# Queries and keys of a sliding-window attention and gated FFN kernel: cast by DMA into 4 KB runs and turned in 32x32 blocks on VectorE

## The chip, the cores and the metric

One core of a Trainium2 chip. The metric is the device time of one execution in microseconds (us). A time is the median of several runs on one chip; the kernel before and the changed kernel were run in turn.

## The reference

Attention over q, k, v of shape (8 batches, 8 heads, 576 tokens, 64 channels) in float32, causal, with a window of 64 tokens; its output, laid out as 4608 tokens x 512 channels, goes through a gated FFN with 1536 hidden channels.

```python
scores = scale * q @ k.T                       # per batch and head
mask   = (rel >= 0) & (rel < 64)               # rel = query position - key position
attn   = softmax(where(mask, scores, -1e9))
x      = (attn @ v).transpose(0, 2, 1, 3).reshape(4608, 512)
out    = (silu(x @ w_gate) * (x @ w_val)) @ w_out
```

## The kernel before

The 4608 tokens are worked in nine tiles of 512 (the tiles cross batch borders, so a tile has one or two segments). The score matmuls read queries and keys with channels on partitions: `qT`, `kT` are 128 partitions (two heads of 64 channels, a "head pair" `u`) x 4 pairs x 512 tokens. The kernel gets there in four steps: SyncE loads float32 with two tokens per partition row, GpSimd casts, TensorE transposes 128x128 blocks against an identity into PSUM (the memory that TensorE's results go to in this kernel; one buffer of 128x512 float32 in it is called a bank here), and ScalarE and VectorE copy the result to SBUF (the memory of all its other tiles).

```python
def cast_qk(t):                                 # GpSimd, 8 casts of 128x512
    ...
def transposes(t, u):                           # 8 transposes on TensorE, 2 copies
    tp = ps_a.tile([P, 2, 512], BF16, name="tp", tag="a")
    ...
    nc.tensor.transpose(tv[:, i, g, e], x[:, g, e, 2*u:2*u+2, :]..., identb[:])
    ...
    nc.scalar.copy(outs[0], parts[0])           # qT
    nc.vector.tensor_copy(outs[1], parts[1])    # kT

def gate_value(t, m):                           # 12 of these per tile
    g_ps = ps_f.tile([P, 512], FP32, name="g_ps", tag="g")   # two buffers
    v_ps = ps_f.tile([P, 512], FP32, name="v_ps", tag="v")   # two buffers
    # 4 + 4 matmuls of 128x512
    nc.scalar.activation(sg[:], g_ps[:], AF.Silu)
    nc.vector.tensor_mul(hT[t][:, m, :], sg[:], v_ps[:])      # frees v_ps

for t in range(2, NT):
    if t > 2:
        loads_qk(t + 2); loads_v(t + 1)         # ends of the range cut
        # attention phase: products(t, u), scores(t + 1, u), project(t - 1, s)
    cast_qk(t + 2)
    for m in range(12):                         # gate/value stage
        gate_value(t, m)
        if m % 3 == 2:
            u = m // 3
            cast_v(t + 1, u)
            masks(t + 1, u)                     # on GpSimd
            transposes(t + 2, u)
```

VectorE runs its instructions in order: in after, an `hT` multiply whose inputs were done by 205.96 us starts at 209.75, behind the mask and the two transposes that stand before it in the program. And the multiply that writes `hT` is the only thing that frees a `v_ps` bank in the gate/value stage, and there are two such banks.

The softmax here doesn't subtract the row's maximum and nothing guards it: scores larger than these inputs give would overflow.

Of the kernel before, what the change touches and what calls it, by code (L numbers as in the profile page):

```python
# [8 lines left out]
P = 128  # L9
FP32 = mybir.dt.float32  # L10
BF16 = mybir.dt.bfloat16
# [6 lines left out]
def kernel(  # L18
# [10 lines left out]
    nc = tc.nc  # L29
    S, D, H = 576, 64, 8  # L30
    NTOK, DFF, DM = 4608, 1536, 512
    NT = NTOK // 512

    ctx.enter_context(tc.manual_schedule())
    cst = ctx.enter_context(tc.tile_pool(name="cst", bufs=1))
    stage = ctx.enter_context(tc.tile_pool(name="stage", bufs=2))
    cast = ctx.enter_context(tc.tile_pool(name="cast", bufs=1))
    att = ctx.enter_context(tc.tile_pool(name="att", bufs=2))
# [6 lines left out]
    wg = cst.tile([P, 4, DFF], BF16, name="wg")  # L45
    wv = cst.tile([P, 4, DFF], BF16, name="wv")
    wo = cst.tile([P, 12, DM], BF16, name="wo")
    kT = [cst.tile([P, 4, 512], BF16, name=f"kT{i}") for i in range(2)]
    vp = [cst.tile([P, 9, H, D], BF16, name=f"vp{i}") for i in range(2)]
    identb = cst.tile([P, P], BF16, name="identb")  # L50
    ones = cst.tile([P, D], BF16, name="ones")
# [2 lines left out]
    def segments(t):  # L54

        n0 = 64 * t
        segs = []
        if n0 > 0:
            segs.append((0, t - 1, S - n0, min(n0, 512)))
        if n0 < 512:  # L60
            segs.append((n0, t, 0, 512 - n0))
        return segs

    staged = {}
# [7 lines left out]
    def load_qk(eng, t, i, h=None):  # L72

        dst = staged[t][i]
        src = (q, k)[i]
        for off, b, s0, n in segments(t):
            o, s, left = off, s0, n
            while left:
                if h is not None and o % 256 == 0 and left >= 256:
                    m, r = left // 256 * 256, P  # L80
                else:
                    m = min(left, 256 - o % 256)
                    r = m // 2
                p0, g = o % 256 // 2, o // 256
                if h is None:
                    eng.dma_start(
                        dst[p0:p0 + r, g].rearrange("r h e d -> r h (e d)"),
                        src[b, :, s:s + m].rearrange("h (r e) d -> r h (e d)", e=2),
                    )
                else:  # L90
                    eng.dma_start(  # L91
                        dst[p0:p0 + r, g:g + max(1, m // 256), h].rearrange("r g e d -> r g (e d)"),
                        src[b, h, s:s + m].rearrange("(g r e) d -> r g (e d)", e=2, r=r),
                    )
                o, s, left = o + m, s + m, left - m

    def load_v(engs, t, by_head=False):

# [40 lines left out]
    def cast_qk(t):  # L139
        casts(t)  # L140
        for g in range(2):
            for e in range(2):
                for i in range(2):
                    cast_unit(nc.gpsimd, t, i, g, e=e)

    def cast_v(t, u):

        v_f = staged[t, "v"]
        hs = slice(2 * u, 2 * u + 2)
        if u == 0 and t:  # L150
            nc.gpsimd.tensor_copy(vp[t % 2][64:128, 0], vp[(t - 1) % 2][64:128, 8])
        for a in range(2):
            r = slice(64 * a, 64 * a + 64)
            dst = vp[t % 2][r, a:a + 8, hs, :].rearrange("r (i c) h d -> r i c (h d)", c=2)
            src = v_f[r, :, hs, :].rearrange("r i h d -> r i (h d)")
            nc.gpsimd.tensor_copy(  # L156
                dst, src.rearrange("r i (c x) -> r i c x", c=1).broadcast_to([64, 4, 2, P])
            )
# [13 lines left out]
    queries = {}  # L172

    def transposes(t, u):
        tp = ps_a.tile([P, 2, 512], BF16, name="tp", tag="a")
        tv = tp[:].rearrange("r i (g j e x) -> r i g e j x", g=2, j=4, e=2)
        for i, x in enumerate(ready[t]):
            for g in range(2):
                for e in range(2):
                    nc.tensor.transpose(  # L180
                        tv[:, i, g, e],
                        x[:, g, e, 2 * u:2 * u + 2, :].rearrange("r h d -> r (h d)"),
                        identb[:],
                    )
        if u == 0:
            queries[t] = att.tile([P, 4, 512], BF16, name="qT", tag="qT")
        parts = [tp[:, i, :].rearrange("r (j e x) -> r j e x", j=8, e=2) for i in range(2)]
        outs = [
            x[:, u, :].rearrange("r (j x e) -> r j e x", j=8, e=2)
            for x in (queries[t], kT[t % 2])  # L190
        ]
        nc.scalar.copy(outs[0], parts[0])  # L192
        nc.vector.tensor_copy(outs[1], parts[1])  # L193

    weights = {}

    def scores(t, u):

        qT = queries[t][:, u, :]
        E = epool.tile([P, 2, 512], BF16, name="E", tag="E")  # L200
        s_ps = [ps_a.tile([P, 512], FP32, name="s_ps", tag="a") for _ in range(2)]
        for j in range(-1 if t else 0, 8):
            c = j % 2
            lo, hi = max(0, 64 * j), min(512, 64 * j + P)
            src = kT[t % 2] if j >= 0 else kT[(t - 1) % 2]
            for h in range(2):
                r = slice(64 * h, 64 * h + 64)
                nc.tensor.matmul(  # L208
                    s_ps[h][64 * c:64 * c + 64, lo:hi],
                    src[r, u, 64 * (j % 8):64 * (j % 8) + 64],  # L210
                    qT[r, lo:hi],
                )
        for h in range(2):
            if t == 0:
                nc.vector.memset(E[64:128, h, 0:64], 0.0)
                nc.scalar.activation(E[0:64, h, 0:64], s_ps[h][0:64, 0:64], AF.Exp, scale=0.125)
            lo = 0 if t else 64
            nc.scalar.activation(E[:, h, lo:512], s_ps[h][:, lo:512], AF.Exp, scale=0.125)  # L218
        weights[t, u] = E

    def masks(t, u, eng=nc.gpsimd):

        E = weights[t, u]
        eng.tensor_mul(  # L224
            E[:].rearrange("r h x -> r (h x)"),
            E[:].rearrange("r h x -> r (h x)"),
            mask[:].rearrange("r h i c x -> r (h i c x)"),
        )
        if 0 < t < 8:
            a = 64 * (1 - t % 2)  # L230
            nc.gpsimd.memset(E[a:a + 64, :, 64 * t:64 * t + 64], 0.0)  # L231
# [41 lines left out]
    def project(t, s, eng=None):  # L273
        o_ps = ps_f.tile([P, 512], FP32, name="o_ps", tag="gv"[s % 2])
        for c in range(12):
            nc.tensor.matmul(  # L276
                o_ps[:], hT[t][:, c, P * s:P * s + P], wo[:, c, :],
                start=(c == 0), stop=(c == 11),
            )
        os_ = fsb.tile([P, 512], FP32, name="os_", tag="os_", bufs=2)  # L280
        if eng is None:
            nc.vector.tensor_copy(os_[:], o_ps[:])
        else:
            nc.scalar.copy(os_[:], o_ps[:])
        nc.sync.dma_start(out[512 * t + P * s:512 * t + P * s + P, :], os_[:])
# [7 lines left out]
    def loads_qk(t):  # L293
        stages(t)
        load_qk(nc.sync, t, 0)
        load_qk(nc.sync, t, 1)

    def loads_v(t):
        load_v((nc.sync, nc.sync), t)
# [62 lines left out]

    attention(1, rest)
    set_silu()
    loads_qk(2)
    loads_v(2)
    for m in range(3):
        gate_value(1, m)
    for s in range(1, 4):
        for t in range(2):  # L370
            for m in range(3 * s, 3 * s + 3):
                gate_value(t, m)
    loads_qk(3)
    loads_v(3)
    cast_qk(2)

    set_exp()
    for u in range(4):
        transposes(2, u)
        if u == 0:  # L380
            project(0, 0)
        scores(2, u)
        cast_v(2, u)
        masks(2, u, nc.vector)
        if u:
            project(0, u)
    cast_qk(3)
    loads_qk(4)
    for u in range(4):
        transposes(3, u)  # L390
        products(2, u)
        project(1, u)
        scores(3, u)
    set_silu()

    for t in range(2, NT):
        if t > 2:
            if t + 2 < NT:
                loads_qk(t + 2)
            if t + 1 < NT:  # L400
                loads_v(t + 1)
            set_exp()
            for u in range(4):
                products(t, u)
                if u % 2 == 0:
                    project(t - 1, u // 2)
            for u in range(4):
                if t + 1 < NT:
                    scores(t + 1, u)
                if u % 2 == 1:  # L410
                    project(t - 1, 2 + u // 2)
            set_silu()
        if t + 2 < NT:
            cast_qk(t + 2)
        for m in range(12):
            gate_value(t, m)
            if m % 3 == 2:
                u = m // 3
                if t + 1 < NT:
                    cast_v(t + 1, u)  # L420
                    masks(t + 1, u)
                if t + 2 < NT:
                    transposes(t + 2, u)
    for s in range(4):
        project(NT - 1, s)

# [29 lines left out]
```

## Time and profile before

| | before |
|---|---|
| median | 402.7 us |
| span of the profiled run | 400.5 us |
| TensorE busy | 352.9 us, 88% |
| VectorE / ScalarE / GpSimd busy | 41% / 48% / 46% |
| first gate matmul of tile 2 | 139.96 us |
| from there to the first gate matmul of tile 7 (five tiles) | 191.7 us, 38.3 each |

How to read the lines: L216 is line 216 of the kernel, an arrow points from what is read to what is written, and xN counts instructions. DVE is VectorE, ACT ScalarE, POOL GpSimd, PE TensorE, PEld its weight loads. The first lines are from the page of before: the span, TensorE's busy time with its share and instructions, and the chain of work that ended last, by engine and by line.

```profile
span 400.5 us, 7241 instructions
PE 352.9 (88%) x2872; PEld 173.4 (43%) x2872; DVE 165.9 (41%) x254; ACT 193.1 (48%) x314; POOL 186.0 (46%) x229
...
PE 76%; POOL 5%; issue 5%; DMA 5%; ACT 4%; SPq 3%; DVE 1%; POOLq 0%; DVEq 0%; ACTq 0%
```

So TensorE is both the busiest engine and three quarters of the chain. The table of windows of before says where it idles. Columns: stretch, its length, then busy us and instruction count of each engine, the granted clock of TensorE (1.00 is full speed), the DMA share and GB/s.

```profile
core 0: us, PE busy (x) PEld busy (x) DVE busy (x) ACT busy (x) POOL busy (x), PEclk, DMA share, GB/s
97.26:121.30 24.04, 16.63 (x162) 8.82 (x160) 9.04 (x13) 8.57 (x14) 11.54 (x18) 0.96 0.19 62
121.30:139.96 18.66, 18.66 (x217) 9.36 (x216) 8.01 (x12) 10.25 (x18) 3.72 (x7) 0.87 0.42 134
139.96:163.20 23.24, 23.24 (x155) 11.65 (x148) 10.82 (x16) 12.15 (x19) 19.58 (x21) 1.00 0.61 148
163.20:179.80 16.60, 15.51 (x183) 7.58 (x182) 6.17 (x9) 12.15 (x20) 13.28 (x17) 1.00 0.14 50
```

The first two rows are the transition from the opening tiles to the steady loop; the third is a gate/value stage, without a gap on TensorE; the fourth is an attention phase, with 1.1 us of gap. (The borders are rough: by the timeline this stage, with its last transposes, goes from 139.96 to 162.48 us, 22.5 us, and the phase to 178.30, 15.8 us.) Whatever leaves TensorE in the third row is saved time (the run packed below bears this out: 22.5 to 20.8 us per stage without the transposes).

The timeline of before, TensorE alone, shows what one group of transposes costs there (start, duration, what):

```profile
303.26 1.03 PE L265 MATMUL v_ps<-xT,wv 128*128 128x512 bf16 x4
304.12 0.39 PE L180 MATMUL tp<-identb,q_b 128*128 128x128 bf16 x4
304.35 0.39 PE L180 MATMUL tp<-identb,k_b 128*128 128x128 bf16 x4
304.57 1.03 PE L265 MATMUL g_ps<-xT,wg 128*128 128x512 bf16 x4
```

Read the starts, not the durations, which overlap: the next gate matmul starts 0.45 us later than it would without the eight transposes. Four groups are 1.8 us per tile.

### The profile page before, as it was taken

The numbers are of one execution on the slowest core, as the hardware profiler recorded it, in microseconds if no ns is written. First come the engines' busy times: TensorE is split into PE (matmuls) and PEld (weight loads), VectorE is DVE, ScalarE is ACT, GpSimd is POOL, SyncE is SP. The second block draws the span as 40 slices with busy tenths as digits, with TensorE's granted clock in tenths as the row PEclk, the third lists the DMA queues.
The fourth block names the chain that finished last, engine by engine and source line by source line (L and its number), as shares of the span: only waits on it lengthen the run. The fifth ranks groups of instructions, "written<-read, shape, count | busy, mean of one in ns | idle before, by whom it ended". The sixth has DMA issues, their size and how long they took to land.

```text
span 400.5 us, 7241 instructions
## 1 busy us (share of the span) xinstructions
PE 352.9 (88%) x2872; PEld 173.4 (43%) x2872; DVE 165.9 (41%) x254; ACT 193.1 (48%) x314; POOL 186.0 (46%) x229
## 2 busy tenths in 40 slices
PE   1368459999669999989999998999899989999996
PEld 0143233444324545445444554445445444444442
DVE  1563534444432544524452544254434433443432
ACT  0476455334424564674476447545663664363320
POOL 7932493200460399778078617952795049000000
PEclk9999559999997999999999999999999999999999
DMA  9693599992117194019212901490160011002002
GB/s 238 170 163 92 139 232 191 204 251 58 54 63 227 54 246 96 29 59 272 64 43 78 285 19 54 130 239 2 54 156 4 0 64 44 0 28 79 2 5 100
DMA packets 87154, 42.94 MB, mean 107 GB/s; under 512 B 40016, under 2 KB 82512, under 8 KB 87120
## 3 DMA queue, kind: packets, MB, share of 16 engines
q1 hardware_dynamic: 77040, 36.19, 34.2%
q0 software_dynamic: 5792, 4.72, 7.5%
q10 hardware_dynamic: 4288, 1.57, 1.5%
q8 instruction: 22, 0.36, 0.4%
q14 instruction: 12, 0.10, 0.1%
HBM read 37.75 MB, written 9.44 MB: 118 GB/s over the span
## 4 chain that ended last, share of the span: by engine, by line
PE 76%; POOL 5%; issue 5%; DMA 5%; ACT 4%; SPq 3%; DVE 1%; POOLq 0%; DVEq 0%; ACTq 0%
PE v_ps L265 23%; PE g_ps L265 23%; PE o_ps L276 22%; PE tp L180 3%; DMA v_f<-in_v_dram 3%; POOL vp L156 2%; PE ad_ps L241 2%; PE s_ps L208 2%; SPq L91 2%; PE ao_ps L245 2%; DMA k_f<-in_k_dram 2%; ACT ld L251 1%; ACT E L218 1%; SPq L109 1%; ACT L288 1%
## 5 line engine op out<-in xcount | busy, mean ns | idle before, releaser
L271 DVE TENSOR_TENSOR hT<-sg,v_ps 128x512 bf16<-128x512 f32 x108 | 74.3, 688 | 103.7 <-PE v_ps L265 101.0
L270 ACT ACTIVATE sg<-g_ps 128x512 f32<-128x512 f32 x108 | 64.4, 597 | 101.8 <-PE g_ps L265 99.7
L265 PE MATMUL g_ps<-xT,wg 128*128 128x512 bf16 x432 | 112.7, 383 | 0.8 <-DVE xT L254 0.8
L265 PE MATMUL v_ps<-xT,wv 128*128 128x512 bf16 x432 | 111.7, 381 | 0.0
L276 PE MATMUL o_ps<-wo,hT 128*128 128x512 bf16 x432 | 100.6, 385 | 0.0
L156 POOL CAST vp<-v_f 64x1024 bf16<-64x1024 f32 x72 | 75.4, 1047 | 16.1 <-DMA v_f<-in_v_dram 13.4
L224 POOL TENSOR_TENSOR E<-E,mask 128x1024 bf16<-128x1024 bf16 x24 | 51.0, 2124 | 32.1 <-ACT E L218 30.6
L265 PEld LDWEIGHTS <-wv 128*128 128x128 bf16 x432 | 42.4, 98 | 53.0 <-issue 2.6
L265 PEld LDWEIGHTS <-wg 128*128 128x128 bf16 x432 | 41.6, 98 | 47.9 <-issue 1.7
L276 PEld LDWEIGHTS <-hT 128*128 128x128 bf16 x432 | 40.2, 99 | 46.8 <-issue 2.5
L218 ACT ACTIVATE E<-s_ps 128x512 bf16<-128x512 f32 (+1 forms) x72 | 38.4, 589 | 24.1 <-PE s_ps L208 23.7
L192 ACT COPY qT<-tp 128x512 bf16<-128x512 bf16 x36 | 26.4, 734 | 39.0 <-PE tp L180 39.0
L132 POOL CAST q_b<-q_f 128x512 bf16<-128x512 f32 x28 | 17.2, 615 | 54.1 <-PE tp L180 30.2
L193 DVE COPY kT<-tp 128x512 bf16<-128x512 bf16 x36 | 26.4, 732 | 37.0 <-ACT qT L192 37.0
L254 DVE TENSOR_TENSOR xT<-ao_ps,r 128x512 bf16<-128x512 f32 x36 | 24.9, 692 | 30.8 <-ACT r L253 30.8
L180 PE MATMUL tp<-identb,q_b 128*128 128x128 bf16 x144 | 16.5, 234 | 15.9 <-POOL q_b L134 13.0
L251 ACT ACTIVATE ld<-ad_ps 128x512 f32<-128x512 f32 x36 | 21.5, 598 | 16.1 <-PE ad_ps L241 14.4
L208 PE MATMUL s_ps<-qT,kT 64*64 64x128 bf16 (+1 forms) x640 | 17.4, 233 | 9.8 <-ACT E L218 4.8
L180 PE MATMUL tp<-identb,k_b 128*128 128x128 bf16 x144 | 16.2, 239 | 11.0 <-DVE k_b L134 11.0
L231 POOL MEMSET E<- 64x128 bf16 x28 | 5.6, 202 | 41.6 <-DVE E L224 40.4
L253 ACT ACTIVATE r<-ld 128x512 f32<-128x512 f32 x36 | 22.7, 630 | 1.2
L180 PEld LDWEIGHTS <-q_b 128*128 128x128 bf16 x144 | 10.7, 101 | 24.4 <-POOL q_b L134 14.4
(65 smaller groups left out, 185.7 us busy)
## 6 DMA issues: line engine op xcount, KB each, us to landing
v_f<-in_v_dram SPq DMA_DIRECT2D x25, 256.0 KB, 5.2
q_f<-in_q_dram SPq DMA_DIRECT2D x9, 512.0 KB, 4.6
k_f<-in_k_dram SPq DMA_DIRECT2D x9, 512.0 KB, 6.2
v_f<-in_v_dram SPq DMA_DIRECT2D x12, 128.0 KB, 3.4
wg<-in_moe_w_gate_dram POOLq DMA_DIRECT2D x4, 384.0 KB, 9.5
wv<-in_moe_w_val_dram POOLq DMA_DIRECT2D x4, 384.0 KB, 11.5
wo<-in_moe_w_out_dram POOLq DMA_DIRECT2D x2, 768.0 KB, 24.3
q_f<-in_q_dram SPq DMA_DIRECT2D x11, 128.0 KB, 3.3
```

Source lines behind the costliest of these rows:

```text
L156: nc.gpsimd.tensor_copy(dst, src.rearrange("r i (c x) -> r i c x", c=1).broadcast_to([64, 4, 2, P]))
L180: nc.tensor.transpose(tv[:, i, g, e], x[:, g, e, 2 * u:2 * u + 2, :].rearrange("r h d -> r (h d)"), identb[:],)
L192: nc.scalar.copy(outs[0], parts[0])
L193: nc.vector.tensor_copy(outs[1], parts[1])
L208: nc.tensor.matmul(s_ps[h][64 * c:64 * c + 64, lo:hi], src[r, u, 64 * (j % 8):64 * (j % 8) + 64], qT[r, lo:hi],)
L218: nc.scalar.activation(E[:, h, lo:512], s_ps[h][:, lo:512], AF.Exp, scale=0.125)
L224: eng.tensor_mul(E[:].rearrange("r h x -> r (h x)"), E[:].rearrange("r h x -> r (h x)"), mask[:].rearrange("r h i c x -> r (h i c x)"),)
L251: nc.scalar.activation(ld[:], d_ps[:], AF.Ln)
L265: nc.tensor.matmul(ps[:], w[:, c, P * m:P * m + P], xT[t][:, c, :], start=(c == 0), stop=(c == 3),)
L270: nc.scalar.activation(sg[:], g_ps[:], AF.Silu)
L271: nc.vector.tensor_mul(hT[t][:, m, :], sg[:], v_ps[:])
L276: nc.tensor.matmul(o_ps[:], hT[t][:, c, P * s:P * s + P], wo[:, c, :], start=(c == 0), stop=(c == 11),)
```

## The change

The intent: take the transposes off TensorE, the casts and masks off GpSimd, and make the DMA runs long. From tile 2 on, GpSimd's DMA queue casts queries and keys to bf16 while it loads them. One partition gets a run of 16 tokens of one head (4 KB of float32). A 32x32 block transpose on VectorE then turns 32 partitions (32 token groups `x`) by 32 channels, once for each of the 16 tokens `e` of a run. Because a block transpose here takes only 32 channels of a run (`src[:, u, :, 0:32]`), each run is loaded twice, for the two channel halves `c`, the second time shifted by 32 elements. The masks move from GpSimd to VectorE.

```diff
+    def load_shifted(t):
+        both = [stage.tile([P, 4, 16, D], BF16, name=n, tag=n) for n in ("q_f", "k_f")]
+        ...
+        w = 16 * D - 32
+        for dst, src in zip(both, (q, k)):
+            for a in range(2):
+                for c in range(2):
+                    for off, b, s0, n in segments(t):
+                        p0 = 64 * a + 32 * c + off // 16
+                        x = src[b, a:H:2, s0:s0 + n].rearrange("u (r e) d -> r u (e d)", e=16)
+                        nc.gpsimd.dma_start(
+                            dst[p0:p0 + n // 16].rearrange("r u e d -> r u (e d)")[:, :, 0:w],
+                            x[:, :, 32 * c:32 * c + w],
+                        )
...
+    def turn(t, u):
+        ...
+        for src, dst in zip(staged[t], (queries[t], kT[t % 3])):
+            nc.vector.transpose(
+                dst[:, u, :].rearrange("r (x e) -> r e x", e=16), src[:, u, :, 0:32]
+            )
...
     for t in range(2, NT):
-                loads_qk(t + 2)
+                load_shifted(t + 2)
...
-            cast_qk(t + 2)
...
-                    masks(t + 1, u)
+                    masks(t + 1, u, nc.vector)
-                    transposes(t + 2, u)
+                    turn(t + 2, u)
```

(Cut: a third `kT` buffer, and the same exchange in the transition, where the four turns of tiles 2 and 3 stand in a row.)

More of the change, by code (lines that the diff above doesn't have):

```diff
@@ L47 @@
     wo = cst.tile([P, 12, DM], BF16, name="wo")
-    kT = [cst.tile([P, 4, 512], BF16, name=f"kT{i}") for i in range(2)]
+    kT = [cst.tile([P, 4, 512], BF16, name=f"kT{i}") for i in range(3)]
     vp = [cst.tile([P, 9, H, D], BF16, name=f"vp{i}") for i in range(2)]
@@ L95, in load_qk @@
                 o, s, left = o + m, s + m, left - m
+    def load_shifted(t):
+        both = [stage.tile([P, 4, 16, D], BF16, name=n, tag=n) for n in ("q_f", "k_f")]
+        staged[t] = both
+        w = 16 * D - 32
[9 more added lines that the diff above has]
+                        )
     def load_v(engs, t, by_head=False):
@@ L189, in transposes @@
             x[:, u, :].rearrange("r (j x e) -> r j e x", j=8, e=2)
-            for x in (queries[t], kT[t % 2])
+            for x in (queries[t], kT[t % 3])
         ]
@@ L193, in transposes @@
         nc.vector.tensor_copy(outs[1], parts[1])
+    def turn(t, u):
+        if u == 0:
+            queries[t] = att.tile([P, 4, 512], BF16, name="qT", tag="qT")
+        for src, dst in zip(staged[t], (queries[t], kT[t % 3])):
+            nc.vector.transpose(
+                dst[:, u, :].rearrange("r (x e) -> r e x", e=16), src[:, u, :, 0:32]
+            )
     weights = {}
@@ L204, in scores @@
             lo, hi = max(0, 64 * j), min(512, 64 * j + P)
-            src = kT[t % 2] if j >= 0 else kT[(t - 1) % 2]
+            src = kT[t % 3] if j >= 0 else kT[(t - 1) % 3]
             for h in range(2):
@@ L364 @@
     set_silu()
-    loads_qk(2)
+    load_shifted(2)
     loads_v(2)
@@ L372 @@
                 gate_value(t, m)
-    loads_qk(3)
-    loads_v(3)
-    cast_qk(2)
+        if s == 1:
+            load_shifted(3)
+            loads_v(3)
+        for u in range(4):
+            if s == 3:
+                cast_v(2, u)
+                turn(2, u)
     set_exp()
     for u in range(4):
-        transposes(2, u)
-        if u == 0:
-            project(0, 0)
         scores(2, u)
-        cast_v(2, u)
         masks(2, u, nc.vector)
-        if u:
-            project(0, u)
-    cast_qk(3)
-    loads_qk(4)
+        project(0, u)
+    load_shifted(4)
     for u in range(4):
-        transposes(3, u)
+        turn(3, u)
+    for u in range(4):
         products(2, u)
@@ L412 @@
             set_silu()
-        if t + 2 < NT:
-            cast_qk(t + 2)
         for m in range(12):
```

## The prediction

> **What bounds the kernel now.** The page: span 400.5 us, TensorE busy 352.9 us (88%); the chain that ended last is 76% TensorE, nearly all gate, value and output matmuls. The table of windows splits the idle: 97.3 to 121.3 us (first scores of tile 2, with projections) has TensorE busy 16.6 of 24.0 us; each later attention phase (163.2 to 179.8) idles 1.1 us, ended by ScalarE's exponentials; the gate/value stages idle nothing. So from 62 us on only work taken off TensorE, or waits in the 97 to 140 stretch, are worth time.
>
> **What the change removes.**
> - TensorE: 8 transposes per head pair from tile 2 on. In the timeline one such group delays the next gate matmul by 0.45 us (304.12 to 304.57), 1.8 us per tile. Tiles 4 to 8 lie in saturated stages: 5 x 1.8 = 9.0 us, all critical.
> - The transition 97.3 to 140.0 (42.7 us): its chain is cast, transpose, ScalarE copy (0.73), VectorE copy (0.73), scores, twice over, and a throttled projection (4.6 us instead of 2.76) after idling. New estimate: 2.2 us wait for the first two VectorE transposes, 4 x 3.1 (scores 0.4, project 2.7), 4 x 3.75 (products, project, scores), 1.5 us for products held by VectorE: 31 us. Gain 11.5 us.
> - GpSimd casts (0.61 us x8 per tile), ScalarE copies and GpSimd masks (2.12 us): off the critical path.
>
> **What it adds.**
> - VectorE: two 32x32-block transposes per head pair, 128x512, costed as the 512-element multiply, 0.69 us ([...]this trace has none yet), plus a 0.69 us mask. Per three gate/value units: 3 x 0.69 + 2.1 = 4.1 us of 5.2. A value eviction is late by about 2 us; two banks absorb it.
> - DMA: queries and keys are read twice (about 4 MB f32 per tile for 2 MB), in 1024 runs of 4 KB. The weight loads, the only cast DMA now, show 5792 packets in 7.5% of 16 engines, 83 ns for 1.5 to 2 KB read; I estimate 160 to 200 ns per 4 KB run, 10 to 13 us per tile of all engines, beside 6 us of values. [...]an issue costs about 0.75 us here, at most eight are in flight by semaphore, 16 per tile. Issue begins with an attention phase; the first transpose is due 16.6 + 5.2 = 21.8 us later. I expect landing after 17 to 22 us: just in time. VectorE runs in order, so a late load holds hT, then TensorE.
>
> **Prediction.** 402.75 - 9.0 - 11.5 + 2 (some late loads) = about 384 us; 8 in 10 between 377 and 397. Faster by over 2% 0.83, within 2% 0.13, slower 0.04.
>
> **What would show it.** Right: transposes 0.6 to 0.75 us; gate/value stages of tiles 2 to 6 take 20.8 us instead of 22.5; second projections start near 111 us; TensorE busy near 337 us, idle 45. Wrong: VectorE's transpose line waits for DMA; TensorE gaps in gate/value stages released by hT; GpSimd held between DMA issues so that tile 2's value casts or mask memsets come after 111 us.
>
> **What would make it wrong.** Runs over 200 ns[...]; block transposes over 1.1 us; doubled reads delaying tile 2 beyond 97 us, as DMA is saturated 50 to 90 us already.

The 0.69 us was an estimate, from the multiply of 512 elements in the trace of before (0.688 us, mean of 108). What the traces show of the rest: the throttled projection (122.36 us in before) ran at a granted clock of 0.59, one of 2.76 us (128.43) at 1.00. An issue took 0.74 to 0.79 us in before (51.62 to 55.28 us). Of the 16 issues from 121.82 us in after, eight go out in a row in 4.06 us, a ninth at 125.95, and each of the other seven waits 0.29 to 1.14 us for a `q_f` load to land. The 6 us of values are near what after shows: a DMA share of 0.91 from 200 to 206 us, 5.5 us by this product, while a tile's values are loaded.

## More of the kernel before

The experiments ran in three groups on three chips (the kernel before took 402.8, 403.4 and 402.0 us there), so a difference between experiments of different groups is good to about 1 us.

## The result, and the profile after

| | before | after |
|---|---|---|
| median of 4 runs each | 402.69 us | 454.52 us |
| span | 400.5 us | 451.2 us |
| TensorE busy | 352.9 us, 88% | 348.8 us, 77% |
| VectorE busy | 165.9 us, 41% | 276.8 us, 61% |
| first gate matmul of tile 2 | 139.96 us | 153.02 us |
| from there to tile 7's, per tile | 38.3 us | 45.9 us |

The ratio is 1.129 (95% interval 1.125 to 1.133). Ratios here are the mean time of one kernel's fast runs over that of the other's of the same rounds, so they are not quite the ratio of the medians quoted. Of the 50.7 us of span, 13.1 came before tile 2's first gate matmul, 37.8 in the five tiles after it, and nothing after that.

The page of after, the same lines:

```profile
span 451.2 us, 6787 instructions
PE 348.8 (77%) x2607; PEld 162.8 (36%) x2648; DVE 276.8 (61%) x306; ACT 173.1 (38%) x286; POOL 161.1 (36%) x253
...
PE 38%; DVE 20%; issue 19%; DMA 15%; POOL 3%; SPq 2%; ACT 1%; DVEq 0%; ACTq 0%; POOLq 0%
```

TensorE has half the share of the chain that it had, and VectorE has 20% of it. The 19% under "issue" belong largely to VectorE as well: in the chain between 203 and 213 us the two long pieces of that name (206.02 to 207.59 and 207.75 to 209.75) lie inside its two transposes. The 15% of DMA are no sign of late loads: they are 16% in the run packed below, which is fast. The groups of after (busy us and mean ns of one, then the idle time of the engine just before them and what ended it):

```profile
L290 PE MATMUL v_ps<-xT,wv 128*128 128x512 bf16 x429 | 114.9, 391 | 27.2 <-DVE hT L296 27.0
L216 DVE STREAM_TRANSPOSE kT<-k_f 128x512 bf16<-128x512 bf16 x28 | 70.5, 2519 | 0.0
L216 DVE STREAM_TRANSPOSE qT<-q_f 128x512 bf16<-128x512 bf16 x28 | 67.1, 2396 | 0.0
```

The transposes take 2.4 to 2.5 us each by their records, not 0.69. They never wait: the idle time before them is 0.0, so the loads are not late. And value matmuls now wait 27 us for `hT`. One third of a gate/value stage in the timeline of after shows how (VectorE and TensorE, two stretches of rows; the last bracket is the idle time before and what ended it):

```profile
204.34 0.69 DVE L296 TENSOR_TENSOR hT<-sg,v_ps 128x512 bf16<-128x512 f32 x1 [1.04 <-PE v_ps L290]
...
204.94 0.69 DVE L249 TENSOR_TENSOR E<-E,mask 128x1024 bf16<-128x1024 bf16 x1
...
205.55 2.39 DVE L216 STREAM_TRANSPOSE qT<-q_f 128x512 bf16<-128x512 bf16 x1
...
207.59 2.49 DVE L216 STREAM_TRANSPOSE kT<-k_f 128x512 bf16<-128x512 bf16 x1
...
209.75 1.44 DVE L296 TENSOR_TENSOR hT<-sg,v_ps 128x512 bf16<-128x512 f32 x2
210.66 1.02 PE L290 MATMUL v_ps<-xT,wv 128*128 128x512 bf16 x4 [2.11 <-DVE hT L296]
...
212.39 0.68 DVE L249 TENSOR_TENSOR E<-E,mask 128x1024 bf16<-128x1024 bf16 x1
```

From 204.94 to 209.75 us VectorE does a mask and two transposes, and no `v_ps` bank comes free. TensorE fills both banks and then stands still for 2.11 us. From mask to mask the third takes 7.45 us; three units of eight matmuls need 5.18. VectorE is busy for 6.86 of the 7.45 us, so its own work alone exceeds the 5.18: by this sum more banks would not have saved the stage (no run tried it). By starts, which is the honest measure for instructions whose records overlap, a transpose costs 2.04 and 2.16 us.

### The profile page after: what moved, and what is told of

It is laid out like the page before. It is cut to its first block, busy times and chain, and to the rows that moved or that the text cites. A ratio compares the mean times of both kernels' runs of the same rounds, so it can differ in the third digit from the quotient of the medians.

```text
span 451.2 us, 6787 instructions
## 1 busy us (share of the span) xinstructions
PE 348.8 (77%) x2607; PEld 162.8 (36%) x2648; DVE 276.8 (61%) x306; ACT 173.1 (38%) x286; POOL 161.1 (36%) x253
## 4 chain that ended last, share of the span: by engine, by line
PE 38%; DVE 20%; issue 19%; DMA 15%; POOL 3%; SPq 2%; ACT 1%; DVEq 0%; ACTq 0%; POOLq 0%
PE o_ps L301 15%; PE v_ps L290 12%; PE g_ps L290 8%; DVE kT L216 7%; DVE qT L216 5%; DMA q_f<-in_q_dram 5%; DVE hT L296 5%; DMA k_f<-in_k_dram 4%; DMA v_f<-in_v_dram 3%; DVE E L249 2%; DMA wv<-in_moe_w_val_dram 2%; POOL vp L172 1%; PE s_ps L233 1%; SPq L91 1%; PE ao_ps L270 1%
## 5 line engine op out<-in xcount | busy, mean ns | idle before, releaser
L290 PE MATMUL v_ps<-xT,wv 128*128 128x512 bf16 x429 | 114.9, 391 | 27.2 <-DVE hT L296 27.0
L290 PE MATMUL g_ps<-xT,wg 128*128 128x512 bf16 x417 | 114.6, 394 | 1.9 <-DVE xT L279 0.8
L216 DVE STREAM_TRANSPOSE kT<-k_f 128x512 bf16<-128x512 bf16 x28 | 70.5, 2519 | 0.0
L216 DVE STREAM_TRANSPOSE qT<-q_f 128x512 bf16<-128x512 bf16 x28 | 67.1, 2396 | 0.0
L290 PEld LDWEIGHTS <-wg 128*128 128x128 bf16 x432 | 43.3, 101 | 54.3 <-issue 6.9
L108 POOL DMA_DIRECT2D q_f<-in_q_dram x52 | 28.8, 567 | 24.0 <-DMA wo<-in_moe_w_out_dram 7.9
L270 PE MATMUL ao_ps<-E,vp 128*64 128x64 bf16 x576 | 17.5, 208 | 22.0 <-DVE xT L279 21.1
L108 POOL DMA_DIRECT2D k_f<-in_k_dram x52 | 28.7, 556 | 11.5 <-DMA q_f<-in_q_dram 10.6
L270 PEld LDWEIGHTS <-vp 128*64 128x64 bf16 x576 | 17.1, 123 | 28.7 <-issue 26.4
L249 DVE TENSOR_TENSOR E<-E,mask 128x1024 bf16<-128x1024 bf16 x36 | 25.2, 701 | 1.6 <-ACT E L243 1.3
```

The lines of the kernel that those rows point to most:

```text
L108: nc.gpsimd.dma_start(dst[p0:p0 + n // 16].rearrange("r u e d -> r u (e d)")[:, :, 0:w], x[:, :, 32 * c:32 * c + w],)
L216: nc.vector.transpose(dst[:, u, :].rearrange("r (x e) -> r e x", e=16), src[:, u, :, 0:32])
L249: eng.tensor_mul(E[:].rearrange("r h x -> r (h x)"), E[:].rearrange("r h x -> r (h x)"), mask[:].rearrange("r h i c x -> r (h i c x)"),)
L270: nc.tensor.matmul(o_ps[64 * h:64 * h + 64, 64 * m:64 * m + 64], vp[t % 2][:, m, 2 * u + h, :], E[:, h, 64 * m:64 * m + 64],)
L290: nc.tensor.matmul(ps[:], w[:, c, P * m:P * m + P], xT[t][:, c, :], start=(c == 0), stop=(c == 3),)
```

## The experiments

Theory A: the write step of 32 bytes makes the transposes three times as long as I took them to be, and VectorE, in order, passes that on through `hT`. Theory B: a bf16 block transpose costs that much in any layout. Theory C: the doubled reads or GpSimd's issuing of them cost the time.

One caution on results. The scores in this problem are so small that the weights inside a window are nearly equal, and the comparison with the reference passed even where I had put tokens in the wrong order. I therefore also compared arithmetic in simulation, without time, with q and k made 12 times larger: the relative error is then 0.006 for before, after and the three versions called right below, and 1.07 for the run with packed writes.

### packed: adjacent writes

```diff
-                dst[:, u, :].rearrange("r (x e) -> r e x", e=16), src[:, u, :, 0:32]
+                dst[:, u, :].rearrange("r (e x) -> r e x", e=16), src[:, u, :, 0:32]
```

> Results wrong on purpose: the block transposes write each 32x32 block as 32 adjacent elements instead of one element every 32 bytes; all else as in the changed kernel. Theory A (the strided write makes a transpose 2.4 us instead of 0.69, and VectorE, in order, then holds the hT evictions): transposes fall to 0.6 to 0.75 us and the time to 380 to 388 us, my predicted value. Theory B (a bf16 block transpose costs 2.4 us in whatever layout): 2.4 us and 454 us stay. Theory C (the doubled reads or the GpSimd issue are what costs; the transposes are long because they wait or contend): the time stays above 430 us whatever the transposes' length.

Measured: 381.47 us, ratio to before 0.948 (0.945 to 0.951). From the page of this run and its groups:

```profile
PE 335.5 (88%) x2648; PEld 158.7 (42%) x2648; DVE 192.4 (51%) x306; ACT 173.1 (46%) x286; POOL 162.2 (43%) x253
...
L216 DVE STREAM_TRANSPOSE qT<-q_f 128x512 bf16<-128x512 bf16 x28 | 19.5, 696 | 0.0
L216 DVE STREAM_TRANSPOSE kT<-k_f 128x512 bf16<-128x512 bf16 x28 | 18.7, 668 | 0.0
```

Nothing changed but the order of the elements within the write, and 73 us went. The loads, their issue, the masks on VectorE and the program on every other engine are as in the changed kernel. Theories B and C fall. It is not a usable kernel, since its tokens are in the wrong order; it is the price list of the rest of the change.

### forms: the step, by size

One form of transpose per tile (destination viewed with `e` = 16, 8, 4, 2, 1, then 1 and 16 with an unbroken source).

> Results wrong on purpose: one form of the transpose per tile. Destination step in elements 16 (tile 2), 8 (tile 3), 4 (tile 4), 2 (tile 5), 1 (tile 6), then step 1 with an unbroken source of 512 elements (tile 7), then step 16 with that source (tile 8). Theory A: 2.4 us at step 16, falling with the step to about 0.65 at step 1 and 2; tile 8 as tile 2, tile 7 as tile 6. Theory B: all 2.4. If the source's half-used rows cost: tiles 7 and 8 about 0.65, the others 2.4.

416.2 us. The timeline of this run, VectorE; two neighbouring transposes each of step 16, 8, 4, 2 and 1:

```profile
101.27 2.50 DVE L222 STREAM_TRANSPOSE kT<-k_f 128x512 bf16<-128x512 bf16 x1
103.42 2.53 DVE L222 STREAM_TRANSPOSE qT<-q_f 128x512 bf16<-128x512 bf16 x1
...
123.98 2.63 DVE L222 STREAM_TRANSPOSE kT<-k_f 128x512 bf16<-128x512 bf16 x1
126.24 2.65 DVE L222 STREAM_TRANSPOSE qT<-q_f 128x512 bf16<-128x512 bf16 x1
...
160.08 1.32 DVE L222 STREAM_TRANSPOSE qT<-q_f 128x512 bf16<-128x512 bf16 x1
161.21 1.33 DVE L222 STREAM_TRANSPOSE kT<-k_f 128x512 bf16<-128x512 bf16 x1
...
197.44 0.74 DVE L222 STREAM_TRANSPOSE qT<-q_f 128x512 bf16<-128x512 bf16 x1
198.09 0.70 DVE L222 STREAM_TRANSPOSE kT<-k_f 128x512 bf16<-128x512 bf16 x1
...
233.76 0.70 DVE L222 STREAM_TRANSPOSE qT<-q_f 128x512 bf16<-128x512 bf16 x1
234.39 0.67 DVE L222 STREAM_TRANSPOSE kT<-k_f 128x512 bf16<-128x512 bf16 x1
```

| write step, bf16 elements (bytes) | start to start, 512 elements |
|---|---|
| 16 (32) | 2.15 us |
| 8 (16) | 2.26 us |
| 4 (8) | 1.13 us |
| 2 (4) | 0.65 us |
| 1 | 0.63 us |
| 1, unbroken source | 0.63 us |
| 16, unbroken source | 2.03 us |

The source plays no part worth naming (0.63 us both ways at step 1, 2.15 and 2.03 at step 16). In this run the cost does not fall in proportion to the step: it is flat up to 4 bytes (0.63 and 0.65 us), about doubles at 8 (1.13), and about doubles again at 16 bytes (2.26), where it stays (2.15 at 32). With step 4 the third of a stage took 5.37 us (mask to mask, 159.48 to 164.85), against 5.18 that TensorE needs: at 1.13 us per transpose VectorE just ceases to be covered.

### masks_pool: the masks back on GpSimd

```diff
-                    masks(t + 1, u, nc.vector)
+                    masks(t + 1, u)
```

> One part undone: the masks of tiles 3 to 8 go back to GpSimd (2.1 us each there instead of 0.69 on VectorE); results right. Theory A: VectorE sets the pace in the five gate/value stages with transposes, so 5 x 4 x 0.69 = 14 us come off: about 440 us, 436 to 446. Theory C (late loads or GpSimd): unchanged or slower, 453 us and up, as GpSimd gets 2.1 us more to do per mask.

Measured: 440.34 us, ratio 1.095 (1.090 to 1.100), with transposes of 2.3 to 2.55 us as before. The expectation held: taking 0.69 us of other work (0.61 start to start) off VectorE 20 times in the five stages gave back 14 us, 12.9 of them from tile 2's first gate matmul to tile 7's, and giving GpSimd 2.1 us more each time cost nothing. VectorE's blocking time is what counts there, within about a microsecond.

### ordered and q_stepped: adjacent writes, the order restored by another engine

In the first, both are transposed into a scratch tile with adjacent writes, and ScalarE copies them into token order a little later. In the second, only keys are copied, and the score matmuls read the queries with the step. (Both cuts are shortened.)

```diff
+            nc.scalar.copy(dst[:, u, :].rearrange("r (x e) -> r x e", e=16),
+                           pk[:, i, :].rearrange("r (e x) -> r x e", e=16))
```

```diff
-                    qT[r, lo:hi],
+                    qT.rearrange("r (e x) -> r x e", e=16)[r, lo // 16:hi // 16, :],   # tiles 2 to 8
```

> A version with right results: the transposes write adjacent elements into a scratch tile, and ScalarE copies queries and keys from it into token order, reading with a step of 64 bytes (8 copies per tile, one third of a stage later). Theory A (only the strided write of the transpose was wrong): transposes 0.7 us, and if ScalarE reads with that step at its usual pace (about 0.73 us a copy, as its copies of 128x512 before), 381 to 386 us, as the run with packed writes. If ScalarE's stepped read costs as VectorE's stepped write did, copies take over 2 us, 17 us per tile, and the time is over 395 us.

> As the ordered version, but the queries stay in the packed order and the score matmuls read them with a step of 64 bytes; only keys are copied by ScalarE. Results right. If TensorE reads a stepped moving operand at full pace: 380 to 384 us, scores group of 18 about 0.42 us as before. If it slows four times as the transposes' writes did: score groups over 1 us, 3 us more per tile, 395 to 405 us.

Measured: ordered 415.77 us (ratio 1.033, 1.028 to 1.037), q_stepped 421.67 us (1.047, 1.043 to 1.051). Both expectations failed in size. The transposes were 0.67 to 0.70 us, as they should be, and ScalarE's stepped copy took 0.95 us start to start, neither 0.73 nor over 2. I had costed the copies by their length and not by their place: they stand in ScalarE's queue ahead of the logarithm that frees a PSUM bank. The timeline of ordered, in the transition (two copies, the logarithm, the matmul that waited):

```profile
122.34 1.04 ACT L228 COPY qT<-pk 128x512 bf16<-128x512 bf16 x1
...
123.29 1.04 ACT L228 COPY kT<-pk 128x512 bf16<-128x512 bf16 x1
...
124.24 0.58 ACT L289 ACTIVATE ld<-ad_ps 128x512 f32<-128x512 f32 x1
...
124.87 0.64 PE L279 MATMUL ad_ps<-E,ones 128*64 128x512 bf16 x2 [5.78 <-ACT ld L289]
```

ScalarE came to 20% of ordered's chain. Against packed, ordered lost 9.4 us before tile 2's first gate matmul and 24 us in the next five tiles, all of it in their attention phases (20.2 to 20.4 us instead of 15.5; the gate/value stages stayed at 20.8). In the first of these phases TensorE waited 2.2 and 0.7 us for the logarithm, and the projection after that took 4.39 us instead of 2.76.

In q_stepped a group of 18 score matmuls took 1.04 to 1.11 us in the transition, where packed had 0.42, and two groups in a row took 1.91 to 1.98 us in the steady loop, where packed had 0.65. The timelines of q_stepped and packed:

```profile
220.25 1.97 PE L248 MATMUL s_ps<-qT,kT 64*64 64x64 bf16 x36
...
162.01 0.65 PE L233 MATMUL s_ps<-qT,kT 64*64 64x64 bf16 x36
```

So these score matmuls pay for a 64-byte step in the queries they read too, about 0.65 us per head pair, some 18 us over 28 head pairs (a sum, not measured apart). How the remaining 22 us over packed divide between the key copies and what follows from them was not taken apart.

### forms2 and forms3: which operations pay

Other operations in the transposes' place, one per tile, results wrong.

> Results wrong on purpose; one other operation per tile in the transposes' place, 128 partitions. Tile 2: VectorE copy of 512 bf16 with a write step of 16 elements; tile 3: the same with step 4; tile 4: the copy with a read step of 16 and adjacent writes; tile 5: ScalarE copy, write step 16; tile 6: block transposes of 256 four-byte elements, write step 32 bytes; tile 7: the same, adjacent writes; tile 8: the bf16 transposes with write step 2. If the cost is VectorE's write path in general: tiles 2 and 3 as the transposes, 2.1 and 1.1 us start to start, tile 4 under 0.7. If it is the transpose alone: tiles 2 to 4 all 0.6 to 0.7. Tile 6 at 1.1 us and tile 7 at 0.35 would say the cost counts elements written[...], not bytes. Tile 5: 0.6 to 0.8 if ScalarE does not share it. Tile 8: 0.65.

> Results wrong on purpose; plain copies in the transposes' place, the same bytes written, 128 partitions. Tile 2: VectorE, 256 four-byte elements, write step 32 bytes; tile 3: the same adjacent; tile 4: VectorE, 512 bf16, write step 16 bytes; tile 5: step 4 bytes; tile 6: adjacent; tile 7: ScalarE, 256 four-byte elements, write step 32 bytes; tile 8: ScalarE, 512 bf16, step 8 bytes. If the cost is that of two-byte writes far apart, on either engine: tile 4 about 2 us start to start, tiles 5 and 6 under 0.5, tiles 2, 3 and 7 under 0.6, tile 8 about 1. If it is the step in bytes whatever the element: tile 2 and 7 about 1 us[...].

400.5 and 380.5 us. From forms2, in order: VectorE's plain copy at a write step of 16 elements, and two neighbouring four-byte transposes at a write step of 32 bytes (timeline, VectorE):

```profile
104.13 2.37 DVE L219 COPY kT<-k_f 128x512 bf16<-128x512 bf16 x1
106.14 2.38 DVE L219 COPY qT<-q_f 128x512 bf16<-128x512 bf16 x1
...
227.81 0.64 DVE L232 STREAM_TRANSPOSE qT<-q_f 128x256 uint32<-128x256 uint32 x1
228.29 0.62 DVE L232 STREAM_TRANSPOSE kT<-k_f 128x256 uint32<-128x256 uint32 x1
```

| operation, 128 partitions, 1 KB per partition | start to start (of two neighbours in a stage, the first) |
|---|---|
| VectorE copy, bf16, write step 16 / 8 / 4 / 2 / 1 elements | 2.01 / 0.90 / 0.57 / 0.34 / 0.21 us |
| VectorE copy, bf16, read step 16, adjacent writes | 0.89 us |
| ScalarE copy, bf16, write step 16 / 4 elements | 1.89 / 1.07 us |
| VectorE transpose, 256 four-byte elements, step 32 bytes / adjacent | 0.48 / 0.36 us |
| VectorE copy, 256 four-byte elements, step 32 bytes / adjacent | 0.23 / 0.20 us |
| ScalarE copy, 256 four-byte elements, step 32 bytes | 0.44 us |

At a step of 32 bytes the cost is not the transpose's: plain copies on VectorE and on ScalarE (2.01 and 1.89 us) pay what the transposes pay (2.15). Four-byte elements at the same byte step pay little: 0.48 us against 0.36 adjacent in the transposes, a third more, and 0.23 against 0.20 in VectorE's copies. Three entries missed. I expected about 2 us for VectorE's copy at a step of 16 bytes, and it took 0.90; 1.1 at a step of 8 bytes, if the write path sets the cost, and it took 0.57; and under 0.7 for the stepped read, and it took 0.89. (0.90 and 0.89 are the first of two neighbours; the second, up to the start of the next multiply, took 1.12 to 1.15.) So a stepped read pays as well, 0.89 us against 0.21, and below 32 bytes copies pay less than transposes do (0.90 us against 2.26 at 16, 0.57 against 1.13 at 8). Why they part there is open.

### pairs: four-byte elements

If two-byte writes far apart are dear (2.15 us for 512 elements 32 bytes apart) and four-byte ones are cheap (0.48 us for 256 at the same step), the block transpose should move pairs of channels. Viewed as 32-bit elements, one token's 64 channels are 32 elements, so one 32x32 block holds a whole head: no second, shifted load, four heads on 128 partitions, and four transposes per tile instead of eight. (My text miscounts the changed kernel's transposes per tile: they are eight.) The two channels of a pair then lie side by side in the free dimension, and the scores become a sum of two matmuls of 32 rows. The keys of tile 1 are turned once more in this form, for the first block of tile 2.

```diff
+            nc.vector.transpose(y.bitcast(U32).rearrange("r (x e) -> r e x", e=16),
+                                src[:, g].bitcast(U32))
...
+            for e in range(2):                  # channel of the pair
+                    r = slice(64 * (u % 2) + 32 * h, 64 * (u % 2) + 32 * h + 32)
+                    nc.tensor.matmul(s_ps[h][...], by_pair(kT, r)[:, keys, e],
+                                     by_pair(qT, r)[:, lo:hi, e], start=(e == 0), stop=(e == 1))
```

> A version with right results: the block transposes move four-byte elements, each a pair of channels, so one 4 KB run per query row group is enough (no second, shifted read: 512 runs per tile instead of 1024) and VectorE does 4 transposes of 512 four-byte elements per tile instead of 16 of 512 two-byte ones in the changed kernel's 8 times 2.1 us; the writes step by 64 bytes. The scores are summed over the two channels of a pair: 36 matmuls of 32 rows per head pair instead of 18 of 64. From the four-byte form just measured (0.48 us start to start for 256 elements at 32 bytes, 0.36 adjacent) I expect 0.8 to 1.0 us a transpose. If the score matmuls of 32 rows run side by side as those of 64 do, or read every second element at full pace: 379 to 386 us. If they take twice the time: 0.35 us more per head pair, 10 us in all, 388 to 394. If four-byte writes at 64 bytes cost as the two-byte ones did, 2 us each: still only 8 us per tile, 382 to 390.

(That score matmuls of 64 rows run side by side can be read from before: a group of 18 holds TensorE 0.35 us, 126.88 to 127.23, for 2048 columns in all, as many as four gate matmuls, which take 0.86 us in turn.)

Measured: 390.12 us (5 runs), ratio to before 0.970 (0.966 to 0.974), results right. Its groups:

```profile
L214 DVE STREAM_TRANSPOSE kT<-k_f 128x512 uint32<-128x512 uint32 x14 | 14.5, 1039 | 0.0
L214 DVE STREAM_TRANSPOSE qT<-q_f 128x512 uint32<-128x512 uint32 x14 | 14.5, 1037 | 0.0
```

A transpose costs 0.85 to 0.91 us start to start, about 0.87, and a group of 36 score matmuls holds TensorE 0.60 us, against 0.34 for packed's 18 (start of the group to start of the next projection). Summed over 28 head pairs, the extra 0.26 us would be 7 us of the 9 between this run and packed; that share was not measured apart. The expectation for score matmuls of twice the time, 388 to 394 us, held. The profile is of the slowest of the five runs (393.31 us): in two of its five attention phases, 18.0 us long instead of 16.4, a projection took 4.22 and 4.01 us instead of 2.76, at a granted clock of 0.59 and 0.62; why is open. It is the best version with right results: faster than before by 3%, and than the changed kernel by 64 us.

## Why the prediction was wrong

- **The step that failed** is the first line under "What it adds": the block transposes "costed as the 512-element multiply, 0.69 us". They measured 2.04 to 2.16 us start to start, 2.4 to 2.5 by their records. The multiply that I took as the model writes adjacent elements; the transposes write 32 bytes apart. With adjacent writes the same transposes are 0.63 us, and the time is 381.5 us, 2.5 below my 384.
- I had the rival in my list ("block transposes over 1.1 us") and gave it almost no weight. The trace of before has no block transpose, so nothing in it showed that one costs what a multiply of as many elements costs, and I measured no stepped write before I predicted. In the forms run the cost is highest and flat from 16 bytes on (2.26 and 2.15 us). The step alone does not explain it: VectorE's copies cost 0.90 us at 16 bytes and 2.01 at 32, and four-byte elements 32 bytes apart pay little (0.48 us for 256, against 0.36 adjacent). The mechanism below the measured step stays open.
- **"A value eviction is late by about 2 us; two banks absorb it"** followed from the same size and fell with it: VectorE frees no bank for 4.8 us (204.94 to 209.75) instead of the 2.1 that I counted, and TensorE stands about 2.1 us in each third. Against packed, the gate/value stage of tile 2 is 27.9 us instead of 20.8, and the attention phase after it 18.0 instead of 15.5: the stage's fourth pair of transposes runs into that phase and holds the multiply for `xT` (TensorE waits 2.3 us for it). The rule itself held where the size was right: in packed VectorE frees no bank for 1.8 us and the gate/value stage has no gap (20.9 us, see below), and I had put the limit at about 1.1 us per transpose, where forms shows the stage just slipping (5.37 against 5.18 us).
- **TensorE's transposes, 9.0 us**: right. Packed against before, tile 2's first gate matmul to tile 7's: 191.7 to 181.6 us, a gain of 10.1. By the timeline, 8.4 of it are in the gate/value stages (22.5 to 20.8 us each) and 1.6 in the attention phases.
- **The transition, 11.5 us**: right. Packed reaches tile 2's gate at 128.86 instead of 139.96 us, a gain of 11.1. In after the four turns in a row hold VectorE from 99.4 to 116.5 us and again from 122.0 to 139.0, and the gate starts at 153.0. TensorE has 0.7 us of work from 129 to 141 us, where its granted clock is 0.50; over the whole stretch the clock is 0.81.
- **Loads just in time, 2 us for late ones**: nothing was late, in no run did a transpose wait for DMA. The estimate of 160 to 200 ns per 4 KB run was close: in packed the cast queue took 32.0% of 16 engines' 379.2 us, 1941 us; less the weights' 481 us (7.5% of 16 x 400.5 in before), 1460 us over 7 x 1024 runs is 204 ns, by this sum.
- **Masks and casts off GpSimd are worth nothing by themselves**: right for the masks in the changed kernel; masks_pool shows that moving them to VectorE cost 14 us while VectorE was the one that blocked. The casts were not tried alone.

The windows of packed, for the transition, a gate/value stage and an attention phase:

```profile
97.54:128.86 31.32, 27.31 (x313) 12.86 (x312) 21.45 (x33) 13.47 (x23) 23.69 (x37) 1.00 0.75 155
128.86:149.75 20.89, 20.89 (x106) 9.39 (x100) 13.04 (x21) 9.63 (x16) 6.81 (x9) 1.00 0.26 64
149.75:165.17 15.42, 14.37 (x193) 7.31 (x193) 7.23 (x11) 10.55 (x18) 10.54 (x19) 1.00 0.82 149
```

These are the 31 us and the 20.8 us that the prediction gave for them. (The border of 149.75 cuts off the start of the attention phase, which is 15.5 us by the timeline.)

## What to carry to other kernels

Cost an operation by the access pattern it will have, not by its element count: two-byte elements written 16 bytes or more apart cost 3.4 times adjacent ones or more in the block transposes here, and 4 to 10 times in VectorE's copies, and the long DMA run on one side of this transpose is what put such a step on the other side. Before you put work on an in-order engine that also frees PSUM banks, first add up whether all its work fits the time of the stage at all, then how long it will free none, and compare that with what the banks can hold. When one term is suspect, a run that makes only that term cheap, with wrong results if need be, tells at once what everything else is worth.
